# A two-branch memory-attention kernel: first weights in two transfers, later betas, one copy per memory-update tile, a new table by slot

## The chip, the cores and the metric

The kernel runs on one core of one Trainium2 chip. A core has a matrix engine (TensorE, "PE" in the profile, with its weight loads as "PEld"), VectorE ("DVE"), ScalarE ("ACT"), GpSimd ("POOL") and SyncE ("SP"), which here only issues transfers. The metric is device time of one launch in microseconds (us); lower is better. Times of several runs are given as their median.

## The reference: what is computed

Two branches, A and B, read the same input x (2048 tokens by 640 features, float32) and have weights of their own. Each cuts the tokens into four segments of 512 and has 32 heads of 20 features. A per-token gate mixes the two outputs.

```python
for s in range(N):                       # N = 4 segments of L = 512
    qs, ks, vs = q[:, :, s], k[:, :, s], v[:, :, s]
    logits = einsum("bhqd,bhkd->bhqk", qs, ks) * scale + mask   # mask: -1e9 where key > query
    p = softmax(logits)
    a_dot = einsum("bhqk,bhkd->bhqd", p, vs)
    pq = phi(qs)                         # phi(t) = t + 1 if t > 0 else exp(t)
    a_mem = einsum("bhld,bhde->bhle", pq, M) / (einsum("bhld,bhd->bhl", pq, z)[..., None] + 1e-6)
    outs.append(g * a_mem + (1.0 - g) * a_dot)       # g = sigmoid(beta), one number a head
    pk = phi(ks)
    M = M + einsum("bhld,bhle->bhde", pk, vs)        # the memory's update
    z = z + pk.sum over tokens
# then o @ wo per branch, and  g_token * A + (1 - g_token) * B
```

So a segment's update of the memory (M with z as a 21st column) is needed by the next segment of the same branch, three times in all for each branch.

## The kernel before, in words

**Stages.** A stage t = 0 to 7 is one segment of one branch (branch t % 2, segment t // 2). Its projections q, k and v take 640 x 640 weights, tiled as 5 x 5 blocks of 128; a projection of one 128-feature tile is 15 products, because every float32 operand is split into a high part and a low part and three of the four combinations are kept (high x high, low weight x high, high x low). Attention goes through 8 quads of 4 heads a stage, 64 quads in all. For a quad, "S" units make the scores with queries on the partitions, whose row maxima VectorE takes (line 1275); "T" units make them again with keys on the partitions, with the maxima as two extra rows, and ScalarE takes the exponential (line 1364) and GpSimd cuts the diagonal block (line 1365); a "PV" unit multiplies with v (line 1392).

**The two ways of using the array.** Projections, S, T, transposes (line 973) and memory reads (line 931) use 64 rows of the array, so two instructions run side by side, one in each half; the planner keeps one queue for each half. PV units and the memory's updates (line 1031) use all rows and 32 columns, four side by side, and both halves have to come to a stop for them. The first two projections (q tile 0 and k tile 0, `job_head`, line 870) and the last ones (line 1217) use the full array.

**The memory's update** (`updates` and `updated`). After a PV unit up to three feature tiles m are updated together: 4 token blocks x 4 windows of 32 features a tile, all three tiles side by side in one PSUM bank of 512 columns, 7 or 8 heads x 21 columns a tile (147 or 168). A window of 32 features meets only 2 or 3 heads, so 42 or 63 columns. VectorE then copies each window out of PSUM (line 1052, four copies a tile), to `mbd` in the first segment and to a scratch tile `mt` (there are two) in later ones; GpSimd zeroes what belongs to other heads (`keep_own_heads`, lines 377 and 381) and, in later segments, adds `mt` to `mbd` (line 1057). The bank is given back when the last of its tiles has been copied. 30 tiles are updated in all, in 12 batches of two or three.

**What sets the order.** The order of all instructions is made while the program is built, by a planner that keeps a model of the engines with a cost for every operation: `put(engine, cost, emit, then, prio)` queues an operation, `dma(...)` a transfer on SP's queue, `Store.want` and `give` hand out buffers (8 PSUM banks, 35 rows of 128 x 512, 3 staging tiles `wst`, 4 pairs `wh`/`wl` of split weights). On the chip each engine runs its own list in order and waits by semaphore, so an operation that takes longer than its cost delays all that stands behind it. The planner counts 0.44 for the copies of one updated tile (in `updated`) and `UPD` = 63 / 1200 + 0.0027 for each of the 8 steps of its products. `RULES` holds one line for each of 66 slots (a slot is about one quad): the order in which the slot's five S and five T units come, and seven numbers: how the units are spread over the slot (`span`), when late work may start (`calm`, `wait`), delays between the two halves (`lag`, `wait2`), how many rows must be free (`room`) and how early the slot begins (`hold`).

**The head of the program.** PE starts with `WARM` = 9 idle products on a zeroed tile (line 356). SP issues, in this order, the whole weight tile of q 0 (320 KB), x tile 0 (256 KB), the weight tile of k 0, x tiles 1 and 2, the two branches' betas, and then x tiles 3 and 4, which reuse rows of x that have been split. ACT rounds each arrival to its high part (lines 559 and 604), DVE makes the low part (lines 557 and 609), and `job_head` multiplies whatever is there. When the betas have come, `head_gates` runs their sigmoids: a chain that goes from ACT to DVE and back twice (lines 644, 645 and 651). GpSimd meanwhile sets constants (`small_tiles`, `ones_tiles`), and zeroes the ten `mbd` and two `mt` tiles (line 373).

Of the kernel before, what the change touches and what calls it, by code (L numbers as in the profile page):

```python
# [18 lines left out]
P = 128  # L19
D = 640  # L20
# [22 lines left out]
def tile_gated_mix_infini_attn(  # L43
# [314 lines left out]
    def warm_up():  # L358

        nc.vector.memset(r32(qst[0][:, 0, :]), 0.0)  # L360
        for _ in range(WARM):
            idle_step()

    WARM = 9

    def ones_tiles():
        for t in vst:
# [1400 lines left out]
    for k in range(KT):  # L1768
        if k < len(HEAD0):
            stage(k)  # L1770
# [88 lines left out]
```

## Time and profile before

| what | value |
|---|---|
| median of 3 runs | 998.64 us (998.44 to 998.71) |
| the profiled execution's own time | 997.83 us |
| its span | 996.1 us |
| busy: PE, PEld, DVE, ACT, POOL | 979.4, 821.2, 814.0, 654.4, 604.5 us |
| PE's products with half the array on projections (line 820) | 5400 |
| copies out of PSUM for updates (line 1052) | 120, of 206 ns on average |

A line of a list of groups or of a timeline names the source line, the engine, the operation, the tile written and the tiles read, the shape and the count; in square brackets stands how long the engine had been idle before, and what ended that. A line of the waits reads: engine and line that waited, what it waited for, total us, times, longest. PE's busy time is the union of overlapping, pipelined products, so a busy PE may still have one half of the array empty.

### The profile page before, as it was taken

To read this page: it belongs to the slowest core of one execution; us is meant where nothing else is said; L and a number is where in the kernel's file an instruction comes from. 1 tells how busy PE (TensorE), PEld (TensorE's weight loads), DVE (VectorE), ACT (ScalarE), POOL (GpSimd) and SP (SyncE) were. 2 spreads that over 40 slices of the span, in tenths; PEclk is the share of its full clock that TensorE was granted. 3 is DMA by queue.
4 is the path that set the end of the run, shared out by engine and by line. 5 is a ranking of instruction groups with operands and counts; after the bars stand their busy time and mean duration, and the time that the engine had idled before them with its cause. 6 is when DMAs were issued, how large, how long until landed. Compare 5 with 4: busy or idle time off the path is not lost.

```text
span 996.1 us, 31535 instructions
## 1 busy us (share of the span) xinstructions
PE 979.4 (98%) x11559; PEld 821.2 (82%) x11559; DVE 814.0 (82%) x2904; ACT 654.4 (66%) x1310; POOL 604.5 (61%) x1052
## 2 busy tenths in 40 slices
PE   9999999999999999999999999999999999999998
PEld 7987888778897888987888877889788987879776
DVE  4796978887798977897879988888788997799874
ACT  5366777676586667685685746776577575675572
POOL 5455656766466765675654676576656664666561
PEclk9999999999999999999999999999999999999999
DMA  7987889898797876976759796789667987887521
GB/s 248 311 281 237 291 234 299 261 279 262 239 307 238 272 214 202 319 241 187 225 173 311 212 283 199 211 270 269 195 214 226 295 279 217 239 251 209 142 90 65
DMA packets 146453, 236.47 MB, mean 237 GB/s; under 512 B 12949, under 2 KB 45882, under 8 KB 145978
## 3 DMA queue, kind: packets, MB, share of 16 engines
q1 hardware_dynamic: 146298, 234.46, 76.4%
q8 instruction: 91, 1.49, 0.6%
q14 instruction: 64, 0.52, 0.2%
HBM read 145.26 MB, written 94.65 MB: 241 GB/s over the span
## 4 chain that ended last, share of the span: by engine, by line
PE 84%; DVE 7%; DMA 4%; issue 2%; POOL 2%; SPq 1%; ACT 1%; DVEq 0%; ACTq 0%; POOLq 0%
PE bank L820 51%; PE bank L1392 13%; PE bank L1288 7%; PE bank L1372 7%; PE bank L973 2%; PE bank L931 2%; DMA row<-dots 1%; DVE mt L1052 1%; DVE bank L1275 1%; DVE mbd L1052 1%; PE bank L1031 1%; DMA row<-rowg 1%; DMA dots<-row 1%; DMA kd<-row 1%; DVE mr L1311 1%
## 5 line engine op out<-in xcount | busy, mean ns | idle before, releaser
L1275 DVE CUSTOM_DVE_ANT_0 bank<-bank,tri 128x384 f32<-128x384 f32 (+3 forms) x1024 | 474.4, 520 | 86.6 <-PE bank L1288 75.0
L820 PE MATMUL bank<-row,wh 64*128 64x512 f32 x2308 | 479.7, 402 | 0.2
L1364 ACT ACTIVATE p<-bank 128x512 f32<-128x512 f32 x550 | 301.5, 605 | 141.5 <-PE bank L1372 113.4
L820 PEld LDWEIGHTS bank<-row,wh 64*128 64x128 f32 x2308 | 308.6, 185 | 16.8 <-PE bank L820 1.8
L1365 POOL TENSOR_SCALAR_AFFINE_SELECT p<-p 128x128 f32<-128x128 f32 (+1 forms) x550 | 203.4, 378 | 188.3 <-ACT p L1364 171.6
L820 PE MATMUL bank<-row,wl 64*128 64x512 f32 x1154 | 292.7, 398 | 0.0
L557 POOL TENSOR_TENSOR wl<-wst,wh 128x640 fp32r<-128x640 f32 x115 | 180.5, 1578 | 61.5 <-ACT wh L559 49.3
L1288 PE MATMUL bank<-kst,qst 60*128 60x384 f32 (+3 forms) x1024 | 174.2, 317 | 6.6 <-DVE mt L1052 2.8
L820 PEld LDWEIGHTS bank<-row,wl 64*128 64x128 f32 x1154 | 172.2, 185 | 7.7 <-issue 1.0
L1372 PE MATMUL bank<-qst,kst 62*128 62x128 f32 (+3 forms) x1024 | 172.8, 319 | 2.3 <-DVE mt L1052 0.9
L820 PE MATMUL bank<-wvh,row 64*128 64x320 f32 (+1 forms) x1280 | 166.0, 312 | 0.6 <-DVE row L770 0.6
L1275 DVE DVE_READ_ACCUMULATOR2_ANT mx<- 128x1 f32 x1024 | 144.4, 141 | 0.2
L1288 PEld LDWEIGHTS bank<-kst,qst 60*128 60x128 f32 x1024 | 128.3, 185 | 18.6 <-DVE mbd L1052 3.9
L820 PEld LDWEIGHTS bank<-wvh,row 64*128 64x128 f32 x1280 | 140.7, 185 | 3.1 <-DVE row L770 0.9
L1392 PE MATMUL bank<-p,vst 128*32 128x384 f32 (+3 forms) x1840 | 141.8, 423 | 0.0
L1372 PEld LDWEIGHTS bank<-qst,kst 62*128 62x128 f32 x1024 | 127.8, 186 | 17.0 <-DVE mx L1275 3.9
L1392 PEld LDWEIGHTS bank<-p,vst 128*32 128x32 f32 x1840 | 57.4, 110 | 82.2 <-issue 58.7
L559 ACT CAST wh<-wst 128x640 fp32r<-128x640 f32 x119 | 86.2, 744 | 34.2 <-PE bank L820 18.8
L820 PE MATMUL bank<-wvl,row 64*128 64x320 f32 (+1 forms) x640 | 99.4, 311 | 0.0
L820 PEld LDWEIGHTS bank<-wvl,row 64*128 64x128 f32 x640 | 80.7, 186 | 0.6 <-issue 0.4
L1311 DVE STREAM_TRANSPOSE mr<-mt 32x32 f32<-32x32 f32 x256 | 51.0, 199 | 26.9 <-POOL mt L1300 24.2
L1423 ACT COPY row<-bank 128x512 f32<-128x512 f32 x58 | 34.4, 594 | 56.4 <-PE bank L1392 51.5
(121 smaller groups left out, 1146.2 us busy)
## 6 DMA issues: line engine op xcount, KB each, us to landing
qst<-qd SPq DMA_DIRECT2D x128, 240.0 KB
kst<-kd SPq DMA_DIRECT2D x128, 240.0 KB
qd<-row SPq DMA_DIRECT2D x40, 512.0 KB
kd<-row SPq DMA_DIRECT2D x40, 512.0 KB
dots<-row SPq DMA_DIRECT2D x56, 256.0 KB
wst<-wmix SPq DMA_DIRECT2D x35, 320.0 KB
row<-dots SPq DMA_DIRECT2D x42, 256.0 KB
qd<-row SPq DMA_DIRECT2D x40, 256.0 KB
```

The source lines that it names most:

```text
L557: put(lo_eng, lo_cost, lambda: lo.tensor_tensor(out=wl, in0=w3, in1=r32(wh), op=ALU.subtract), end, prio=3)
L559: put("A", 0.625, lambda: nc.scalar.copy(wh, w3), low, prio=6)
L820: return nc.tensor.matmul(bank_of, lhsT=w[ROWS[half]], rhs=x_[ROWS[half]], start=start, stop=stop)
L931: return nc.tensor.matmul(pm[:, a - h0:c - h0, :].rearrange("p h e -> p (h e)"), lhsT=r32(pqTs[t, m][ROWS[half], P * n:P * (n + 1)]), rhs= ...
L1275: put("D", w / 960.0 + 0.105, lambda: nc.vector.tensor_tensor_reduce(out=sc[:, off:off + w], in0=sc[:, off:off + w], in1=tri[:, L - w:], s ...
L1288: lane_ops[half].append((mm(w), lambda pair=pair, qb=qb, off=off, w=w, r=r, sc=sc: nc.tensor.matmul(sc[:, off:off + w], lhsT=q[r, pair, P ...
L1311: nc.vector.transpose(r32(mr[:, 32 * j:32 * j + 32]), r32(mt[32 * j:32 * j + 32, :]))
L1364: put("A", 0.483, lambda: nc.scalar.activation(pt, sc, AF.Exp, scale=SCALE), lambda: (bank.give(sc), put("G", 0.15 + 0.105 * len(todo), la ...
L1365: "G", 0.15 + 0.105 * len(todo), lambda: nc.gpsimd.affine_select(out=blocks, in_=blocks, pattern=[[0, len(todo)], [1, P]], base=0, channel ...
L1372: lane_ops[half].append((mm(w), lambda pair=pair, kb=kb, off=off, w=w, r=r, sc=sc: nc.tensor.matmul(sc[:, off:off + w], lhsT=k[r, pair, P ...
L1392: nc.tensor.matmul(po[32 * j:32 * j + 32, P * kb:], lhsT=vst[t % 2][:, kb, h * E1:h * E1 + 32], rhs=pts[i, n, f][0][:, off:off + w], start ...
L1423: either(0.483, lambda: nc.scalar.copy(r32(oT), po), 0.605, lambda: nc.vector.tensor_copy(r32(oT), po), end, 2)
```

## The change

- **Weights of the head in two transfers each.** `head_weights` brings k-block 0 of a tile (128 x 128, 64 KB) by itself, into a row, and blocks 1 to 4 (256 KB) into a staging tile. SP's order is now: q 0 first piece, x tile 0, k 0 first piece, q 0 rest, x tile 1, k 0 rest, x tile 2, x tiles 3 and 4. Each piece is split by itself. `job_head` takes its weights from `head_hi` and `head_lo`; the rows go back when a projection is done.
- **Two idle products fewer**: `WARM` = 7.
- **The betas** are asked for at 16.0 of the planner's clock, not at the start. Their chain of sigmoids moves with them.
- **One copy for each updated tile**: the whole tile (128 partitions x 147 or 168 columns) is copied at once, whatever the other heads' places in PSUM hold, and `keep_own_heads` zeroes those as before. The copy is counted at 0.22, `UPD` at 0.047, and the twelve tiles are no longer zeroed at the start (`ones_tiles` is counted at 1.6, not 2.8).
- **All 66 lines of `RULES` but one are new.** The planner makes another order from them, on every engine; what is multiplied is the same.

```diff
-        1: "SSTSTSTSTT 1.01 2.38 0.34 8 1.4 1.6 1",
+        1: "TSTSTSTSTS 1.01 2.38 0.3 8 0 1.6 1.12",
...
-    WARM = 9
+    WARM = 7
...
-        for t in (*mbds[0], *mbds[1], *mt_store.free):
-            nc.gpsimd.memset(t, 0.0)
...
+    def head_weights(i, part):
+        t, kind, m = jobs[i]
+        src = weights[t % 2][kind][m]
+        staged.add(i)
+
+        def split_from(w3, wh, wl, us, hi_us, lo_us, end):
+            def landed():
+                def low():
+                    head_hi[i, part] = wh
+                    put("D", lo_us, lambda: nc.vector.tensor_tensor(out=wl, in0=w3, in1=r32(wh), op=ALU.subtract), end, prio=3)
+
+                put("A", hi_us, lambda: nc.scalar.copy(wh, w3), low, prio=6)
+
+            cols = slice(0, 1) if part == 0 else slice(1, KT)
+            dma(us, lambda: nc.sync.dma_start(out=w3, in_=src[:, cols, :]), landed, prio=0, lat=1.1)
+
+        if part == 0:
+            def got_rows(*rows):
+                head_rows[i] = rows
+                st, wh, wl = (x[:, :P].rearrange("p (k n) -> p k n", k=1) for x in rows)
+
+                def end():
+                    head_lo[i, 0] = wl
+
+                split_from(r32(st), wh, wl, 0.25, 0.2, 0.2, end)
+
+            big.want((F32, F32R, F32R), got_rows)
+            return
...
-    UPD = 63 / 1200.0 + 0.0027
+    UPD = 0.047
...
-        def take(dst):
-            for r, a, c in windows(m):
-                h = slice(a - LO[m], c - LO[m])
-                nc.vector.tensor_copy(dst[r, h, :], v[r, h, :])
...
-            put("D", 0.44, lambda: take(tmp), lambda: (
+            put("D", 0.22, lambda: nc.vector.tensor_copy(tmp[:, :nh, :], v), lambda: (
...
-            put("D", 0.44, lambda: take(mbd), lambda: (
+            put("D", 0.22, lambda: nc.vector.tensor_copy(mbd, v), lambda: (
...
-    for k in range(KT):
-        if k < len(HEAD0):
-            stage(k)
+    for i in (0, 1):
+        head_weights(i, 0)
+        if i == 0:
+            want_x(0, 0)
+    for i in (0, 1):
+        head_weights(i, 1)
+        want_x(0, 1 + i)
+    for k in (3, 4):
         want_x(0, k)
...
-        dma(0.9, lambda b=b: nc.sync.dma_start(out=bts[b], in_=betas[b].partition_broadcast(P)), betas_there, prio=15)
+        at(16.0, lambda b=b: dma(0.9, lambda: nc.sync.dma_start(out=bts[b], in_=betas[b].partition_broadcast(P)), betas_there, prio=15))
```

**How the order changes.** Engine lists are shown in program order, with the line of the kernel (of the changed one, where lines moved: 870 became 909, 820 became 858, 1275 became 1310, 1052 became 1094 and 1099).

On ACT before, at the head of the program: the beta chain (`gmem`, `gdot`, `gcol`, line 644) stands ahead of the rounding of x tiles 3 and 4.

```order
L604 CAST row_25_197<-row_6_190 128x512
L644 ACTIVATE gmem_92<-beta_199 128x32
L644 ACTIVATE gdot_94<-beta_199 128x32
L644 ACTIVATE gcol_132<-gcol_132 128x1
L644 ACTIVATE gmem_93<-beta_200 128x32
L644 ACTIVATE gdot_95<-beta_200 128x32
L644 ACTIVATE gcol_133<-gcol_133 128x1
L604 CAST row_72_233<-row_4_188 128x512
L604 CAST row_77_236<-row_7_191 128x512
```

On ACT now, from its first rounding on: the two small weight pieces (written to rows 10 and 21), the two larger ones (`wh`), and all five x tiles (line 642), with nothing else between them.

```order
L582 CAST row_10_191<-row_9_190 128x128
L642 CAST row_16_194<-row_4_186 128x512
L582 CAST row_21_197<-row_20_196 128x128
L582 CAST wh_145<-wst_142 128x512
L642 CAST row_29_199<-row_5_187 128x512
L582 CAST wh_147<-wst_143 128x512
L642 CAST row_37_201<-row_6_188 128x512
L642 CAST row_84_222<-row_4_186 128x512
L642 CAST row_89_225<-row_7_189 128x512
```

The six instructions of the beta chain have gone from between the third and the fourth x tile; they now stand behind the second k projection's evacuation.

On DVE before, at the update of tiles 2, 3 and 4 in the first segment of branch A: eleven rows for the twelve copies and, behind them, the first row maximum of the next S unit.

```order
L1052 COPY mbd_2_72<-bank_141 32x63
L1052 COPY mbd_2_72<-bank_141 32x42 x2
L1052 COPY mbd_2_72<-bank_141 32x63
L1052 COPY mbd_3_73<-bank_141 32x42
L1052 COPY mbd_3_73<-bank_141 32x63
L1052 COPY mbd_3_73<-bank_141 32x42 x2
L1052 COPY mbd_4_74<-bank_141 32x63
L1052 COPY mbd_4_74<-bank_141 32x42
L1052 COPY mbd_4_74<-bank_141 32x63
L1052 COPY mbd_4_74<-bank_141 32x42
L1275 ISA bank_137,mx_1640<-bank_137,tri 128x512
```

On DVE now, at the same update:

```order
L824 TENSOR_TENSOR row_1510_1510<-bank_135,row_1509_1509 128x512
L1346 STREAM_TRANSPOSE mr_161<-mt_1531 32x32 x4
L1099 COPY mbd_2_72<-bank_137 128x168
L1099 COPY mbd_3_73<-bank_137 128x147
L1099 COPY mbd_4_74<-bank_137 128x147
L1310 ISA bank_137,mx_1614<-bank_137,tri 128x512
```

Twelve copies have become three, and the bank that the next S unit takes is the one that they empty.

On PE before, ahead of the fourth PV unit from the end: two projections (banks 2 and 0) side by side, one in each half of the array, and an S unit (banks 7 and 1) in both halves.

```order
L820 MATMUL bank0_134<-row23_17920_15547,wh3_151 128x512
L1288 MATMUL bank7_141<-kst2_86,qst2_82 128x256
L1288 MATMUL bank1_135<-kst2_86,qst2_82 128x256
L1288 MATMUL bank7_141<-kst2_86,qst2_82 128x256
L1288 MATMUL bank1_135<-kst2_86,qst2_82 128x256
L820 MATMUL bank2_136<-row23_17920_15547,wl2_150 128x512
L820 MATMUL bank0_134<-row23_17920_15547,wl3_152 128x512
L820 MATMUL bank2_136<-row5_17921_15548,wh2_149 128x512
L820 MATMUL bank0_134<-row5_17921_15548,wh3_151 128x512
L820 MATMUL bank2_136<-row12_17934_15560,wh2_149 128x512
```

On PE now, at about the same place (bank 6 collects a projection, bank 1 transposes of the memory's output O, banks 3 and 0 a T unit):

```order
L858 MATMUL bank6_140<-row19_18077_15553,wh1_147 128x512
L858 MATMUL bank6_140<-row19_18077_15553,wl1_148 128x512
L1013 MATMUL bank1_135<-ident_68,O0_157 128x64 x4
L858 MATMUL bank6_140<-row14_18078_15554,wh1_147 128x512
L858 MATMUL bank6_140<-row7_18044_15528,wh1_147 128x512
L858 MATMUL bank6_140<-row7_18044_15528,wl1_148 128x512
L1407 MATMUL bank3_137<-qst0_80,kst0_84 128x256 x2
L1407 MATMUL bank0_134<-qst0_80,kst0_84 128x256 x2
L858 MATMUL bank6_140<-row26_18045_15529,wh1_147 128x512
L858 MATMUL bank6_140<-row34_18061_15541,wh1_147 128x512
```

Here one projection's products follow each other in one half of the array, with four short transposes as their only company in the other.

More of the change, by code (lines that the diff above doesn't have):

```diff
@@ L554, in split_hi @@
                 wh, wl = pair
-                def low():
-                    split_hi_[i] = pair
-                    put(lo_eng, lo_cost, lambda: lo.tensor_tensor(out=wl, in0=w3, in1=r32(wh), op=ALU.subtract), end, prio=3)
-                put("A", 0.625, lambda: nc.scalar.copy(wh, w3), low, prio=6)
+                put("A", 0.625, lambda: nc.scalar.copy(wh, w3), lambda: put(
+                    lo_eng, lo_cost,
+                    lambda: lo.tensor_tensor(out=wl, in0=w3, in1=r32(wh), op=ALU.subtract), end, prio=3), prio=6)
                 def end():
@@ L570, in stage, with got, end @@
         wst.want(1, got, prio=i)
+    head_hi, head_lo, head_rows = {}, {}, {}
+    def head_weights(i, part):
[19 more added lines that the diff above has]
+            return
+        def got(w, pair):
+            def end():
+                wst.give(w)
+                split[i] = pair
+                head_lo[i, 1] = pair[1][:, 1:, :]
+            w3 = w.rearrange("p (k n) -> p k n", n=P)
+            split_from(w3[:, 1:, :], pair[0][:, 1:, :], pair[1][:, 1:, :], 0.84, 0.52, 0.62, end)
+        wst.want(1, lambda w: whl.want(1, lambda pair: got(w, pair), prio=i), prio=i)
     mixed_there = set()
@@ L856, in there @@
             k, i, j = x
-            return i in (split if j == 1 else split_hi_) and (0, k) in (xs if j == 2 else x_hi)
+            return (i, min(k, 1)) in (head_lo if j == 1 else head_hi) and (0, k) in (xs if j == 2 else x_hi)
         while todo:
@@ L874, in job_head @@
             if n[i] == 3 * KT:
+                big.give(*head_rows.pop(i))
                 after_whole(qk_finish(*jobs[i], pps[i]))
```

9 lines of the change are left out of this document (5 added, 4 removed), and 128 rows, old and new, of the table RULES.

## The prediction

> **What bounds the kernel now.** I read the page first, then the busy time by window, the waits of PE, the lines that copy updates out of PSUM, and timelines of one update and of the head. The page's span and busy times, and one window:
>
> ```profile
> span 996.1 us, 31535 instructions
> PE 979.4 (98%) x11559; PEld 821.2 (82%) x11559; DVE 814.0 (82%) x2904; ACT 654.4 (66%) x1310; POOL 604.5 (61%) x1052
> ...
> 30.00:60.00 30.00, 30.00 (x299) 28.56 (x297) 26.08 (x105) 15.40 (x35) 13.09 (x17) 1.00 0.92 297
> ```
>
> PE has something in flight in all but 17 us, so nothing but PE can set the end, and a microsecond that PE saves early is kept: the window from 30 to 60 shows no idle time in which it could get lost. But "busy" is a union; one half of the array may be empty in it. What PE waited for (engine and line, released by, total us, times, longest):
>
> ```profile
> PE bank L1288 <- DVE mt L1052: 2.8, 3, 1.2
> PE bank L1288 <- DVE mbd L1052: 2.8, 3, 1.7
> ...
> PE bank L1288 <- DVE row L776: 1.0, 1, 1.0
> PE bank L1372 <- DVE mt L1052: 0.9, 2, 0.5
> PE bank L870 <- ACT row L604: 0.8, 2, 0.6
> PE bank L820 <- DVE row L770: 0.6, 1, 0.6
> PE bank L1372 <- DVE mbd L1052: 0.6, 1, 0.6
> ```
>
> Of the 9.5 us in these rows, line 1052, the copies of updates, holds 2.8 + 2.8 + 0.9 + 0.6 = 7.1, and line 604, x in the head, 0.8. Both are what the change touches. One update of three tiles, in the timeline (start, length, engine, line, tiles, count; in brackets the idle time before and its releaser):
>
> ```profile
> 92.40 1.36 PE L1031 MATMUL bank<-vst,row 128*32 128x63 f32 x96
> ...
> 93.84 2.67 DVE L1052 COPY mbd<-bank 32x63 f32<-32x63 f32 x12 [3.38 <-PE bank L1031]
> ...
> 96.56 0.30 PEld L1288 LDWEIGHTS bank<-kst,qst 60*128 60x128 f32 x4 [2.12 <-DVE mbd L1052]
> 96.56 0.50 PE L1288 MATMUL bank<-kst,qst 60*128 60x384 f32 x4 [1.69 <-DVE mbd L1052]
> ```
>
> The planner counted 3 x 0.44 = 1.32 for these twelve copies and got 2.67. It had promised the bank to an S unit (line 1288), and PE stood 1.69 until the last copy.
>
> **The copies (term 1).** Durations of DVE operations that read PSUM, by group (busy us, mean ns), and a later update, whose third tile needs a scratch tile back from GpSimd:
>
> ```profile
> L948 DVE TENSOR_TENSOR O<-bank,mw 128x320 f32<-128x320 f32 x48 | 23.6, 491 | 1.7
> ...
> L1052 DVE COPY mt<-bank 32x42 f32<-32x42 f32 (+1 forms) x80 | 16.5, 206 | 8.4 <-PE bank L1031 4.8 <-issue 1.2 <-POOL mbd L1057 0.7
> ...
> L989 DVE COPY row<-bank 128x512 f32<-128x512 f32 x6 | 4.1, 689 | 2.0 <-PE bank L973 2.0
> ```
>
> ```profile
> 468.54 0.54 POOL L1057 TENSOR_TENSOR mbd<-mbd,mt 128x168 f32<-128x168 f32 x1
> ...
> 469.11 0.93 DVE L1052 COPY mt<-bank 32x63 f32<-32x63 f32 x4 [0.73 <-POOL mbd L1057]
> ...
> 470.10 0.44 PE L1288 MATMUL bank<-kst,qst 60*128 60x384 f32 x1 [0.99 <-DVE mt L1052]
> ```
>
> From 320 to 512 columns the time grows by (689 - 491) / 192 = 1.03 ns a column, so a copy of 147 columns should take about 491 - 173 x 1.03 = 313 ns and one of 168 about 335, by estimate. Three take 0.96, not 2.67: 1.7 earlier, which is the longest wait. In a later segment the third copy still waits for GpSimd; there the first copy ends 0.93 - 0.31 = 0.6 earlier and so does GpSimd's work, and the third is 0.6 shorter: 1.2 earlier, again the longest wait of `mt`. Had the order stayed, all 7.1 would go. What may stay: the planner now counts 0.22 for what should take 0.31 to 0.34, so a batch of three is still promised 0.3 too early; over the 9 stops of the four rows that is 2.7 at most, and 4.4 are saved. What may be saved beyond: the weight loads of one half waited longer than PE as a whole.
>
> ```profile
>   PEld bank L1288: 7.5, 6
> ...
>   PEld bank L1372: 2.8, 4
> ```
>
> That is 10.3 in all. So the copies give -7.1, within -4.4 and -10.3; I take the row of PE itself. DVE is freed of 120 x 0.206 - 30 x 0.32 = 15 us, and what comes late next at such a place is GpSimd's zeroing, which no row shows PE waiting for. The smaller `UPD` only moves the planner's clock: 96 products took 1.36, so 0.43 to 0.45 a tile, beside 8 x 0.055 = 0.44 counted before and 8 x 0.047 = 0.38 now. That promises a bank up to 0.2 earlier a batch, and is in the 2.7.
>
> **The head (term 2).** PE's idle products (line 356), the head's products (line 870), and what ACT and SP did:
>
> ```profile
> 3.39 2.33 PE L356 MATMUL bank<-qst 128*128 128x512 f32 x5
> 5.88 0.80 PE L870 MATMUL bank<-row,wh 128*128 128x512 f32 x1 [0.16 <-ACT row L604]
> ...
> 6.90 1.21 PE L870 MATMUL bank<-row,wh 128*128 128x512 f32 x4
> ...
> 10.53 0.40 PE L870 MATMUL bank<-row,wh 128*128 128x512 f32 x1
> 11.53 0.50 PE L870 MATMUL bank<-row,wh 128*128 128x512 f32 x1 [0.60 <-ACT row L604]
> ...
> 12.56 0.86 PE L870 MATMUL bank<-row,wh 128*128 128x512 f32 x3
> ```
>
> ```profile
> 0.81 0.38 SPq L568 DMA_DIRECT2D wst<-in_a_wq_dram  x1
> ...
> 1.25 0.42 SPq L624 DMA_DIRECT2D row<-in_xT_dram  x1
> ...
> 4.10 0.73 ACT L559 CAST wh<-wst 128x640 fp32r<-128x640 f32 x1 [2.02 <-DMA wst<-in_a_wq_dram]
> ...
> 5.21 0.62 ACT L604 CAST row<-row 128x512 fp32r<-128x512 f32 x1 [0.38 <-DMA row<-in_xT_dram]
> ...
> 8.02 0.23 ACT L644 ACTIVATE gmem<-beta 128x32 f32<-128x32 f32 x1
> ...
> 9.97 0.20 ACT L644 ACTIVATE gcol<-gcol 128x1 f32<-128x1 f32 x1 [1.60 <-DVE gcol L651]
> ...
> 10.87 1.12 ACT L604 CAST row<-row 128x512 fp32r<-128x512 f32 x2
> ```
>
> x tile 0 (256 KB) was there 1.11 after the 320 KB ahead of it. With 64 KB ahead it should come 1.1 earlier: rounding at 4.1, PE's first product at 4.8, not 5.88. Seven idle products cover that: the nine end at about 5.5, two fewer at 4.7. At first PE is slow: five idle products in 2.33 are 0.42 apart, while three of the head at 12.56 are (0.86 - 0.40) / 2 = 0.23 apart; the four from 6.90 are (1.21 - 0.40) / 3 = 0.27 apart, so the change falls near 7.1. Before it three products had started (5.88 to 6.90), now six: 3 x 0.23 = 0.7 saved. Second, the stop from 10.53 to 11.53: x tiles 3 and 4 were rounded at 10.87, behind the beta chain, which held ACT from 8.02 and waited 1.60 for DVE in it. Without it a step of 0.23 remains: 0.8 saved, if the tiles have landed. They were asked for when x tile 0's row was free, so they too come 1.1 earlier, at 9.8 at the latest, rounded by 10.4; PE would want them at about 10.1. Term 2 is -1.5; without the second part -0.7, with both unreduced (1.1 + 0.8) -1.9.
>
> The Trainium skill (TensorE: Matmul & The Clock Gate, "What's actually happening") says that PE's clock is gated to half until one free-running window of about 3.4 us has been busy, and falls back after an idle one. The spacings, 0.42 and then 0.23, agree with it; by that rule fewer idle products are no gain, and a gap after them a risk (a rival below).
>
> The beta chain now stands on ACT and DVE behind the second k projection, about 3 us long, with two weight roundings and that projection's own low part behind it on their queues. Before, the first of those roundings stood idle for its transfer:
>
> ```profile
> 25.05 0.73 ACT L559 CAST wh<-wst 128x640 fp32r<-128x640 f32 x1 [0.67 <-DMA wst<-in_a_wq_dram]
> ```
>
> So ACT has slack there, PE is full with projections (the window from 30 to 60 above), and I count nothing; if the cover fails, PE waits for that rounding, 3 - 0.67 = 2.3 at worst, and I leave 0.5 of it in the range. The 12 zeroings taken from GpSimd were behind everything that PE needs. The gate's small transfer keeps its place behind the weights; its products stand at the end of the head.
>
> **The table (term 3).** PE's order has the same products as before, two idle ones aside, so the table can only change how well the two halves are filled. Two rows each of full projections price a product in one half:
>
> ```profile
> 20.29 1.33 PE L820 MATMUL bank<-row,wl 64*128 64x512 f32 x10
> ...
> 21.46 1.32 PE L820 MATMUL bank<-row,wh 64*128 64x512 f32 x10
> ...
> 24.86 1.99 PE L820 MATMUL bank<-wvh,row 64*128 64x322 f32 x24
> ...
> 26.68 0.91 PE L820 MATMUL bank<-wvl,row 64*128 64x322 f32 x10
> ```
>
> Ten of 512 columns take 1.17 in two halves, 0.234 each in its half; 24 of 322 take 1.82, 0.152 each. That is 0.011 + 0.00044 x columns. Adding this up in PE's order for each half between two PV units, the fuller half exceeds the mean of both by 4.6 us in all before, and by 8.1 now; 2.4 of the difference lies in the two stretches ahead of the fourth and third PV unit from the end, where one projection runs alone. So +3.5 at most by this count. At the other end: kinds of instruction change inside a half 2615 times, not 2661, and if each change costs 0.1 (no row isolates it), that is 46 x 0.1 / 2 = -2.3; a table made for the new costs may also leave out the other stops of the waits (1.0 + 0.6), so -4. I take +1.5: I halve the count and round down, because a half that is thin in the order may be so at a place where PE would have waited anyway.
>
> **Sum.** -7.1 - 1.5 + 1.5 = -7.1. The profiled execution took 997.83 (span 996.1 and 1.7 around it): 990.7. The median of the runs, 998.64, is 0.8 above it: 991.5.
>
> **The rivals.** (a) *The bank is still late.* The third copy of a batch stands on DVE waiting for GpSimd, with the row maxima of the next S unit behind it; for it is the 0.73 above, and a DVE order in which the next S unit takes the very bank; against it, that stop was part of the waits already counted. Half of term 1 stays: 991.5 + 3.6 = 995.1. (b) *The clock opens a window later,* since x comes after the seven idle products end and PE pauses. Eight more products at 0.42 in place of 0.23 cost 8 x 0.19 = 1.5, so 993.0; against it, transfers should be there at 4.1. By the Trainium skill's window (the same page and section), half speed for 3.4 us more, it would be 1.7 by estimate. (c) *The table fits better than the count says,* its -4 end: 991.5 - 5.5 = 986.0. (d) *Slower: the new order bunches units at the end of the program,* where few projections are left, and PE stops for PSUM banks that DVE's maxima or ACT's exponentials hold. A stop costs up to 1.7 (the longest above). Eight of them in the last ten stretches make 13.6: 991.5 + 13.6 = 1005. From five stops on (7.1 / 1.7 = 4.2) the change is a loss. For it: the two thin stretches, DVE at 82%. Against: the freed 15 us of DVE. (e) That a copy of 128 partitions costs four times one of 32 is excluded by line 948, 128 partitions at 491 ns.
>
> **How the numbers follow.** Forecast 0.62, (a) 0.13, (b) 0.05, (c) 0.08, (d) 0.12. The time is the forecast's. Its own range, from the terms' ends not all at once, is 987 to 996. With (a) to (c) and the far end of term 1 (3.2 more) in part, the range is 985 to 997.5; it leaves out (d) and all far ends at once. A measurement of this kernel tells about 0.2%, 2.0 us, from no change: faster is below 996.6, slower above 1000.6. Faster: 0.62 x 0.97 + 0.13 x 0.75 + 0.05 x 0.9 + 0.08 = 0.82. Slower: (d) in two of three cases, 0.08. Same: 0.10.
>
> **What would show it.** PE's first head product near 4.8 and no stop of a microsecond ahead of x tile 3; lines 1094 and 1099 at about 320 ns each and gone from the list of what PE waits for, or below 1 us in all; PE's waits otherwise at 4 us or less. I am wrong if the new order brings waits of another kind that add up to more than 3 us, if the copies take over 0.5, or if the head's first product stays near 5.9.

## The result, and the profile after

The changed kernel took 991.81 us (median of 4, 990.02 to 994.29) beside 998.67 us for the kernel before (998.44 to 999.74): a ratio of 0.9931 [0.9907, 0.9955]. Timed again beside the last two experiments it took 993.61 us, 0.9949 [0.9937, 0.9962]. The forecast was 991.5. The experiments show that this was luck: two errors cancelled, one of 7 us and one of 8 to 9. The copies alone are worth 14 us, and the rest of the change costs 8 to 9.

The profiled execution, 994.29 us, was the slowest of its four. Its page, and after it the list of what PE waited for as a whole (engine and line, released by, total us, times, longest):

```profile
span 992.5 us, 31438 instructions
...
PE 981.9 (99%) x11557; PEld 824.9 (83%) x11557; DVE 804.1 (81%) x2826; ACT 648.1 (65%) x1299; POOL 603.5 (61%) x1043
```

```profile
PE bank L356 <- DVE qst L360: 1.5, 1, 1.5
PE bank L1013 <- issue: 1.4, 1, 1.4
PE bank L909 <- ACT row L642: 0.9, 2, 0.7
PE bank L1323 <- DMA kst<-kd: 0.9, 1, 0.9
PE bank L1323 <- ACT p L1399: 0.5, 2, 0.4
PE bank L971 <- DVE mx L1310: 0.4, 1, 0.4
```

The copies have left the list, as forecast. PE's span shrank by 3.6 us, yet it is busy 2.5 us longer than before with two products fewer. That is a first hint that a busy PE has got emptier. A second profile of the same kernel shows it too: 982.1 busy in a span of 991.3.

The copies of the kernel after by group, and one of its updates in the timeline:

```profile
L1094 DVE COPY mt<-bank 128x147 f32<-128x147 f32 (+1 forms) x20 | 5.5, 310 | 10.2 <-PE bank L1071 8.3 <-POOL mbd L1092 1.9
...
L1099 DVE COPY mbd<-bank 128x147 f32<-128x147 f32 (+1 forms) x10 | 2.6, 309 | 5.1 <-PE bank L1071 5.1
```

```profile
92.16 1.36 PE L1071 MATMUL bank<-vst,row 128*32 128x63 f32 x96
...
93.67 0.77 DVE L1099 COPY mbd<-bank 128x168 f32<-128x168 f32 x3 [1.21 <-PE bank L1071]
...
94.49 0.26 PEld L1323 LDWEIGHTS bank<-kst,qst 60*128 60x128 f32 x2 [0.52 <-DVE mbd L1099]
```

A copy takes 310 and 309 ns (forecast 313 to 335). But copies in a row overlap: each starts 0.22 to 0.25 us after the one before. So three take 0.77 (forecast 0.96), where the new planner counts 0.66, and a batch of two takes 0.53, where it counts 0.44. A batch is promised only 0.1 too early. The products of three tiles still take 1.36, and the weight load of the next S unit waits for the last copy: 0.52, no longer 2.12, but not nothing.

The head of the kernel after in the timelines of PE and of ACT:

```profile
4.77 2.23 PE L909 MATMUL bank<-row,row 128*128 128x512 f32 x6
7.68 0.51 PE L909 MATMUL bank<-row,wh 128*128 128x512 f32 x1 [0.68 <-ACT row L642]
...
8.31 1.20 PE L909 MATMUL bank<-row,wh 128*128 128x512 f32 x4
...
11.18 0.50 PE L909 MATMUL bank<-row,wh 128*128 128x512 f32 x1 [0.26 <-ACT row L642]
...
14.27 0.39 PE L909 MATMUL bank<-row,wh 128*128 128x512 f32 x1
```

```profile
7.01 0.62 ACT L642 CAST row<-row 128x512 fp32r<-128x512 f32 x1 [0.59 <-DMA row<-in_xT_dram]
...
10.50 1.26 ACT L642 CAST row<-row 128x512 fp32r<-128x512 f32 x2 [1.63 <-DMA row<-in_xT_dram]
```

PE starts at 4.77 (forecast 4.8), and then stands for x tile 1 and again for x tiles 3 and 4, which ACT had to wait 1.63 us for. The last product of the head starts at 14.27; in the kernel before it did so at 14.19:

```profile
14.19 0.40 PE L870 MATMUL bank<-row,wh 128*128 128x512 f32 x1
```

So the head gained nothing in this profile. Its end differs from run to run: with the old head the last product started at 13.74 to 14.29 in five profiles of different kernels, and in the second profile of the kernel after at 13.73. No gain shows over that spread.

### The profile page after: what moved, and what is told of

Read it like the earlier page. It is cut to its first block, busy times and chain, and to the rows that moved or that the text cites. A ratio compares the mean times of both kernels' runs of the same rounds, so it can differ in the third digit from the quotient of the medians.

```text
span 992.5 us, 31438 instructions
## 1 busy us (share of the span) xinstructions
PE 981.9 (99%) x11557; PEld 824.9 (83%) x11557; DVE 804.1 (81%) x2826; ACT 648.1 (65%) x1299; POOL 603.5 (61%) x1043
## 4 chain that ended last, share of the span: by engine, by line
PE 92%; DMA 3%; DVE 3%; issue 1%; ACT 1%; SPq 0%; ACTq 0%; DVEq 0%
PE bank L858 55%; PE bank L1427 14%; PE bank L1323 8%; PE bank L1407 8%; PE bank L971 3%; PE bank L1013 2%; PE bank L1071 1%; DMA kst<-kd 1%; DMA row<-in_xT_dram 1%; DMA beta<-in_b_beta_dram 1%; DMA kd<-row 1%; DVE bank L1310 1%; PE bank L1252 0%; DMA qd<-row 0%; DVE row L1237 0%
## 5 line engine op out<-in xcount | busy, mean ns | idle before, releaser
L858 PE MATMUL bank<-row,wh 64*128 64x512 f32 x2308 | 485.9, 402 | 0.1
L858 PEld LDWEIGHTS bank<-row,wh 64*128 64x128 f32 x2308 | 313.0, 185 | 16.6 <-PE bank L858 0.9
L1400 POOL TENSOR_SCALAR_AFFINE_SELECT p<-p 128x256 f32<-128x256 f32 (+1 forms) x544 | 199.6, 377 | 183.0 <-ACT p L1399 169.8
L858 PE MATMUL bank<-row,wl 64*128 64x512 f32 x1154 | 297.3, 398 | 0.0
L858 PE MATMUL bank<-wvh,row 64*128 64x320 f32 (+1 forms) x1280 | 179.4, 313 | 0.0
L1407 PE MATMUL bank<-qst,kst 62*128 62x384 f32 (+3 forms) x1024 | 171.9, 317 | 0.1
L1323 PE MATMUL bank<-kst,qst 60*128 60x384 f32 (+3 forms) x1024 | 170.1, 319 | 1.7 <-DMA kst<-kd 0.9
L858 PEld LDWEIGHTS bank<-wvh,row 64*128 64x128 f32 x1280 | 148.8, 185 | 1.6 <-issue 0.6
L1427 PE MATMUL bank<-p,vst 128*32 128x512 f32 (+3 forms) x1816 | 139.5, 424 | 0.0
L1323 PEld LDWEIGHTS bank<-kst,qst 60*128 60x128 f32 x1024 | 124.3, 186 | 14.8 <-issue 2.0
```

Source lines behind the costliest of these rows:

```text
L858: return nc.tensor.matmul(bank_of, lhsT=w[ROWS[half]], rhs=x_[ROWS[half]], start=start, stop=stop)
L1323: lane_ops[half].append((mm(w), lambda pair=pair, qb=qb, off=off, w=w, r=r, sc=sc: nc.tensor.matmul(sc[:, off:off + w], lhsT=q[r, pair, P ...
L1400: "G", 0.15 + 0.105 * len(todo), lambda: nc.gpsimd.affine_select(out=blocks, in_=blocks, pattern=[[0, len(todo)], [1, P]], base=0, channel ...
L1407: lane_ops[half].append((mm(w), lambda pair=pair, kb=kb, off=off, w=w, r=r, sc=sc: nc.tensor.matmul(sc[:, off:off + w], lhsT=k[r, pair, P ...
L1427: nc.tensor.matmul(po[32 * j:32 * j + 32, P * kb:], lhsT=vst[t % 2][:, kb, h * E1:h * E1 + 32], rhs=pts[i, n, f][0][:, off:off + w], start ...
```

## The experiments

### One copy per tile in the old order

```diff
-            for r, a, c in windows(m):
-                h = slice(a - LO[m], c - LO[m])
-                nc.vector.tensor_copy(dst[r, h, :], v[r, h, :])
+            nc.vector.tensor_copy(dst[:, :nh, :], v)
```

This is the kernel before with nothing else changed: same table, same counts, same head, same order on every engine.

> The kernel before, with its own order of work, its old table and its old head; only the copies of an updated tile out of PSUM are one each instead of one per head's window. The planner still reckons 3 x 0.44 = 1.32 us for a batch whose copies should now take about 0.96, so no bank is promised too early. My theory (the copies were waited for, and nothing else takes their place): 998.6 - 7.1 = 991.5, ratio 0.993, and neither mt nor mbd stands in the list of what PE waits for with more than 0.5 us. Rival, the bank is late anyway because GpSimd's zeroing and adding stand behind the copies: half of it, 995 (0.9965). Rival, the gain of the change came from the new table: no more than 2 us here, 997 (0.998).

Measured: 983.88 us, 0.9859 [0.9845, 0.9872]. That is 14 us, twice my theory, and better than the whole change. Its page, and the update that the prediction showed for the kernel before, in the timeline:

```profile
span 982.2 us, 31441 instructions
...
PE 973.5 (99%) x11559; PEld 823.6 (84%) x11559; DVE 792.7 (81%) x2814; ACT 653.7 (67%) x1310; POOL 602.9 (61%) x1052
```

```profile
91.18 1.36 PE L1031 MATMUL bank<-vst,row 128*32 128x63 f32 x96
...
92.63 0.77 DVE L1050 COPY mbd<-bank 128x168 f32<-128x168 f32 x3 [3.39 <-PE bank L1031]
...
93.45 0.30 PEld L1286 LDWEIGHTS bank<-kst,qst 60*128 60x128 f32 x4 [0.22 <-DVE mbd L1050]
93.45 0.50 PE L1286 MATMUL bank<-kst,qst 60*128 60x384 f32 x4
```

The same 11559 products keep PE busy 5.9 us less (979.4 to 973.5), and its idle time falls by 8.0 (from 996.1 - 979.4 = 16.7 to 8.7). Nearly all of the 5.9 lies in the stretches with an update, busy by the page, and in no list of what PE waited for. I read it as time in which one half of the array stood for the bank while the other half worked. That is not shown, since no view keeps the halves apart. There is another reading: a product's record is longer than the distance to the next product (0.39 beside 0.23 us in the head), so every stop also adds a tail that counts as busy.

Since both kernels have the same order, the starts of their PV units can be subtracted one by one. The difference grows almost only around the updates and stays nearly flat between them, and it is 14.0 us at the 63rd of the 64. Six of the 12 batches have three tiles and ran over their promise by 2.67 - 1.32 = 1.35. The other six have two tiles, whose eight copies took 1.76 for 0.88. Together that is 6 x 1.35 + 6 x 0.88 = 13.4, about the 14.0 that were paid. (This counts the copies' own time. In later segments the third copy of a batch waits for GpSimd as well, with one copy a tile as with four.) Against the planner's own clock (the time its code holds when it places a PV unit) the picture is plain. Chip minus planner, us:

```
PV unit                    1st   11th   31st   41st   63rd
planner, old table        62.2  194.8  494.1  643.9  959.6
  before                   0.8    6.2    8.7   11.2   14.5
  one copy                 0.4    0.1   -0.8   -0.8    0.5
  copied twice             0.8    2.9    3.7    4.5    6.6
planner, new table        65.2  192.1  498.1  642.8  955.1
  after                    3.0    3.8    6.9   10.0   11.1
  after, second run        2.1    2.8    4.1    8.8   10.0
  after, thin copies       1.9    1.8    2.7    6.7    7.8
  the same, fewer products 3.4    2.4    3.0    4.7    5.5
```

With one copy the chip follows the plan to within 1 us through 960 us. The kernel before fell behind it by 14.5, and the kernel after falls behind its own plan by 10 to 11 again.

### Each tile copied twice

```diff
             nc.vector.tensor_copy(dst[:, :nh, :], v)
+            nc.vector.tensor_copy(dst[:, :nh, :], v)
```

> The kernel before with one copy per updated tile, and that copy made twice in a row (the same data, no result changes). Three tiles then hold DVE for 6 x 0.31 = 1.87 us where the planner promises 3 x 0.44 = 1.32: late by 0.55 a batch, after 1.35 with the four copies (2.67) and -0.36 with one. The theory now (what counts is by how much a batch runs over what the planner promised, nearly all of it is paid, 14.0 us for 12 batches that ran over by 1.35): 12 x 0.55 = 6.6, less the 0.18 a batch that the 14.0 fell short of 12 x 1.35, so 4.4 to 6.6 above the 983.9 of one copy: 988.3 to 990.5, ratio 0.9904 to 0.9926. Rival (PE has projections to fill in, only a lateness of about a microsecond is felt): within 1 us of one copy, 0.985 to 0.987.

Measured: 989.95 us, 0.9912 [0.9897, 0.9928], inside the theory's 0.9904 to 0.9926; the rival is out. The same update in its timeline:

```profile
93.17 0.33 DVE L1050 COPY mbd<-bank 128x168 f32<-128x168 f32 x1 [3.38 <-PE bank L1031]
...
94.68 0.31 DVE L1051 COPY mbd<-bank 128x147 f32<-128x147 f32 x1
...
95.05 0.30 PEld L1287 LDWEIGHTS bank<-kst,qst 60*128 60x128 f32 x4 [1.28 <-DVE mbd L1051]
95.05 0.50 PE L1287 MATMUL bank<-kst,qst 60*128 60x384 f32 x4 [0.84 <-DVE mbd L1051]
```

Six copies end 1.8 us after the first began, where 1.32 was promised, and the S unit that was given the bank is late. The four copies of a batch of two took 1.22 for 0.88, so the batches ran over by 6 x 0.50 + 6 x 0.34 = 5.0 in all, and 6.1 were paid. (My theory had taken all twelve batches for batches of three, here and for the 14.0.) What a batch costs is by how much it runs over its promise, even when that is half a microsecond.

### Four copies in the new order

The kernel after with the four windows of a tile copied singly again, and the scratch tiles zeroed at the start.

```diff
-            put("D", 0.22, lambda: nc.vector.tensor_copy(mbd, v), lambda: (
+            put("D", 0.22, lambda: take(mbd), lambda: (
```

> The kernel after in its own order, but each updated tile is copied window by window again (and the scratch tiles are zeroed at the start, as that needs). The planner reckons 3 x 0.22 = 0.66 us for a batch whose copies take 2.7, so banks are promised 2.0 us too early, 1.35 before the change. My theory (the copies decide): the 7.1 us of waits come back and grow by the difference of promises, about 0.65 x 9 stops = 6, so between +7 and +13 on the 991.8 of the kernel after: 999 to 1005, ratio to the kernel before 1.000 to 1.006. Rival (the table or the head made the gain, copies matter little): below 995, ratio under 0.9965.

Measured: 1008.71 us, 1.0108 [1.0094, 1.0122]. That is 15 to 17 us above the kernel after, more than expected. A batch of three now runs over by 2.67 - 0.66 = 2.0, one of two by 1.76 - 0.44 = 1.3, together 20, and the chip ends 24.6 us behind the planner at the 63rd PV unit. The copies decide in the new order too.

### The old table under the new counts, and 0.43 for 0.44

The kernel after with the 66 lines of the old table, and nothing else:

```diff
-        1: "TSTSTSTSTS 1.01 2.38 0.3 8 0 1.6 1.12",
+        1: "SSTSTSTSTT 1.01 2.38 0.34 8 1.4 1.6 1",
...
```

> The kernel after with the old table of order and spacing by slot; costs, head, betas and copies stay as changed. My theory from counting lanes (the new table costs 1.5): 990.3, ratio 0.9916. Rival 1 (the table was made for the new costs and pays): 993 or more, ratio above 0.9943, with more waits of PE than the kernel after has. Rival 2 (a table only scatters the order; any table gives the same): within 1 us of the kernel after, 0.9921 to 0.9941.

Measured: 1064.64 us, 1.0660 [1.0637, 1.0683]. My theory and rival 2 fall. Rival 1 holds by its words, 993 us or more with more waits of PE (27 us idle by the page, 10.6 in the kernel after), but nobody had 70 us. The planner's own clock says it too: 1041.5 at the end, beside 978.4 with the new table and 979.1 for the kernel before. What the engines did there, by windows (length; busy us and count of PE, PEld, DVE, ACT, POOL; granted clock, DMA share, GB/s), and the line of its page:

```profile
120.00:125.00 5.00, 5.00 (x67) 5.00 (x64) 4.45 (x22) 4.85 (x10) 3.88 (x7) 1.00 1.05 358
...
135.00:140.00 5.00, 5.00 (x51) 5.00 (x49) 0.00 (x0) 0.83 (x2) 0.00 (x0) 1.00 0.02 3
...
165.00:170.00 5.00, 4.69 (x41) 4.19 (x37) 0.00 (x0) 0.00 (x0) 0.50 (x1) 1.00 1.00 237
```

```profile
PE 1036.3 (97%) x11557; PEld 856.5 (81%) x11557; DVE 799.5 (75%) x2828; ACT 649.5 (61%) x1301; POOL 600.4 (56%) x1039
```

In the windows from 135 and from 165 PE runs 51 and 41 products in 5 us instead of 67, with DVE and ACT nearly idle, and yet counts as busy for 5.00 and 4.69 us. I read that as projections without attention work to pair with. A change of one count by 0.01 does the same to the other table. One copy in the old order, counted at 0.43 (in both places):

```diff
-            put("D", 0.44, lambda: take(mbd), lambda: (
+            put("D", 0.43, lambda: take(mbd), lambda: (
```

> One copy per updated tile in the old order's table, but the planner counts 0.43 us for it instead of 0.44, nothing else. By its own clock the planner now ends at 1032.1 instead of 979.1: the table's numbers were found for 0.44, and everything behind the first update is placed anew. Theory (a table belongs to one set of counts; the chip follows the planner's clock): 983.9 + 53 = 1037, ratio 1.035 to 1.042. Rival (the planner's clock is wrong for such a plan, the chip hardly notices): 984 to 995, ratio under 0.997.

Measured: 1052.04 us, 1.0518 [1.0494, 1.0541]: 68 us for a hundredth of a microsecond in a count. The theory holds in kind, but the time lies above its range: the chip stays within 0.7 us of the plan for the first 24 PV units and falls behind later. So each of these tables belongs to the one set of counts that it was found for, and the worth of "the table alone" cannot be measured by swapping it.

### Shorter copies and fewer products in the new order

```diff
-            put("D", 0.22, lambda: nc.vector.tensor_copy(mbd, v), lambda: (
+            put("D", 0.22, lambda: nc.vector.tensor_copy(mbd[:, :1, :], v[:, :1, :]), lambda: (
...
-            for n in range(NB):
+            for n in range(NB - 1):
```

The first pair of lines (and its like for `mt`) makes the thin copies; the second kernel has both pairs.

> The kernel after in its own order, but each copy of an updated tile takes only the first head's 21 columns of 147 or 168 (the rest of the update is left out, so the memory is not the reference's), and the scratch tiles are zeroed at the start. By 1.03 ns a column the copy should take 0.31 - 0.13 = 0.18 us, under the 0.22 that the planner promises. The theory now (the promise of 0.22 is what costs the kernel after its gain): three copies end 0.39 us earlier, about 12 batches, so 4 to 5 us gained on the kernel after, 987 to 988, ratio 0.989. Rival (the copies are out of the way already, and the loss against one copy in the old order is the new table's filling of the halves): within 1 us of the kernel after, 0.992 to 0.994.

> As the thin copies, and of an update's four products per head window only three are made (a quarter of the update's sum is left out too). 96 products took 1.36 us, 0.45 a tile, where the planner now counts 8 x 0.047 = 0.376; 72 should take 1.02, 0.34 a tile. The theory (both promises are too short): 30 tiles x 0.11 = 3.4 less work on PE beyond the thin copies' gain, 983.5 to 985, ratio 0.986, and PE no longer falls behind the planner's clock at the updates; of the 11 us by which the kernel after ends behind that clock only the 3 of the head and the first stretch are left. Rival (table): 3.4 less work and nothing else, 988.4, ratio 0.990.

Measured: 990.92 us, 0.9924 [0.9911, 0.9936], and 987.71 us, 0.9899 [0.9883, 0.9915]. Both lie where the rival put them. By the medians the thin copies gain 0.9 to 2.7 us (on the kernel after's two times), and the 3.4 us of products left out gain 3.2 more (2.5 by the ratios). The copies did fall under the promise (groups of the thin copies' kernel):

```profile
L1096 DVE COPY mt<-bank 128x21 f32<-128x21 f32 x20 | 2.9, 176 | 10.4 <-PE bank L1073 8.3 <-POOL mbd L1094 1.9 <-issue 0.2
```

So the short promise of the copies is between a tenth and a third of the 8 to 9 us that the kernel after lost. That agrees with what whole copies run over: 6 x 0.11 + 6 x 0.09 = 1.2. The theory had missed that copies in a row overlap. The lag behind the planner between the first and the 63rd PV unit tells the rest: 8 in the kernel after, 6 with thin copies, 2 with fewer products as well. But of that last step 3.4 is work that was really removed; the planner was short of it by 30 x (1.36 / 3 - 0.376) = 2.3.

### The head and the betas

The kernel after, with every instruction in its place but the betas: their transfers go out at the planner's time 50, their chain runs at 64.

```diff
+    at(50.0, lambda: [nc.sync.dma_start(out=bts[b], in_=betas[b].partition_broadcast(P)) for b in range(2)])
+    at(64.0, head_gates)
```

> The kernel after, each instruction in its place but two groups: the two transfers of beta are issued at the planner's time 50 instead of 16, and the chain of gates that reads them stands at 64 on the engines. In the trace of the kernel after, the issue of the betas took SP 1.19 + 0.85 us, and the second landed at 25.9; the S unit of the second half pair began at 44.26 behind a wait for its k tile's transfer, 42.00 in the kernel before. My theory (the betas' place holds up the k tile that goes through DRAM): that S unit starts about 2 us earlier and 1 to 2.5 us are gained, 989.3 to 990.8, ratio 0.9907 to 0.9922. Rival, PE has other work there and loses nothing: same as the kernel after, 991.8 (0.9931). Rival, the chain at 64 meets the maxima of the softmax on DVE and ACT: 1 to 2 us slower than after.

Measured: 993.93 us, 0.9958 [0.9946, 0.9971], no better than the kernel after. In the kernel after, the S unit of the second half pair started late, behind its k tile:

```profile
44.26 0.77 PE L1323 MATMUL bank<-kst,qst 60*128 60x512 f32 x5 [0.94 <-DMA kst<-kd]
```

In this experiment it started at 43.47 with no stop. That need not come from the betas: in the second profile of the kernel after, with nothing moved, it started at 43.28 and had no stop either. And the chain now held ACT ahead of the first PV unit (two rows of its timeline):

```profile
68.05 0.20 ACT L682 ACTIVATE gcol<-gcol 128x1 f32<-128x1 f32 x1 [0.35 <-DVE gcol L689]
...
68.62 0.64 PE L1427 MATMUL bank<-p,vst 128*32 128x512 f32 x4 [1.12 <-ACT vst L1129]
```

A second try put the chain where ACT is idle and gave x tiles 3 and 4 space of their own.

```diff
+    x_fresh = {3: 0, 4: 1}
+            st = O_store.free[0][:, x_fresh[k], :L] if not s and k in x_fresh else row
...
+    at(30.0, lambda: [nc.sync.dma_start(out=bts[b], in_=betas[b].partition_broadcast(P)) for b in range(2)])
+    at(41.5, head_gates)
```

> The kernel after, each instruction in its place but for two things: x tiles 3 and 4 of the head are staged in space of their own, so that their transfers are issued without a wait for rows to come free (SP stood 2.66 us for them); and the two beta transfers are issued at the planner's time 30 and their chain runs at 41.5, where ACT has 5 us free. Theory for the head (the wait for rows is what made x tiles 3 and 4 late, landed at 10.5): both are rounded by 9.8, the head's last product starts 0.5 to 0.8 earlier than 14.27. Rival for the head (the transfers share the queues, an earlier issue only makes them share sooner): landed at 10.2 or later, no gain. For the betas: the S unit of the second half pair starts by 42.5 instead of 44.26, nothing else waits. Together 1.5 to 2.5 us: 989.3 to 990.3, ratio 0.991 to 0.992; by the rival less than 1 us.

Measured: 993.55 us, 0.9949 [0.9935, 0.9962]: nothing gained. The timelines of ACT and of PE in its head:

```profile
8.14 0.62 ACT L582 CAST wh<-wst 128x512 fp32r<-128x512 f32 x1 [0.68 <-DMA wst<-in_a_wk_dram]
8.78 0.62 ACT L646 CAST row<-row 128x512 fp32r<-128x512 f32 x1
9.44 1.31 ACT L646 CAST row<-O 128x512 fp32r<-128x512 f32 x2
```

```profile
14.21 0.39 PE L913 MATMUL bank<-row,wh 128*128 128x512 f32 x1
```

x tiles 3 and 4 are rounded 1.06 us earlier (9.44), as the theory said, and the head ends at 14.21 instead of 14.27, as the rival said: the rest of k's weights came later in exchange (rounded at 8.14, not 7.64). But one profile says little here. In the second profile of the kernel after, unchanged, the two tiles were rounded from 9.97 and the head ended at 13.73. The S unit started at 42.67, 1.6 earlier than in the kernel after, and the first PV unit at 67.90, only 0.3 earlier. In seven runs of this order that PV unit lay anywhere from 66.4 to 68.6. My theory of the betas falls with it: there was a stop (0.94), but not in every run, and moving the betas gained no time.

### Both kernels again, and the best one

> The kernel after once more, unchanged, on the chip that runs the two below, for a narrower interval: 990 to 994, ratio 0.991 to 0.9955. If the first stretch's loss hangs on when the second beta lands, this profile's first PV unit lies anywhere from 66.4 to 68.6 us.

Measured: 993.61 us, 0.9949 [0.9937, 0.9962]; the first PV unit at 67.23. Its profile shows a stop of PE of 1.91 us, the longest in it. Four more runs of this order have that stop at 1.4 us or more, the kernel after's first profile has it at 0.4, and the one with fewer products not at all. ACT waits for a transfer to free a row, and the exponentials behind it hold a bank (timelines of ACT and of PE):

```profile
642.57 0.58 ACT L1029 COPY row<-bank 128x512 f32<-128x512 f32 x1 [2.74 <-DMA kd<-row]
643.05 1.09 ACT L1399 ACTIVATE p<-bank 128x512 f32<-128x512 f32 x2
```

```profile
643.70 0.51 PE L1323 MATMUL bank<-kst,qst 60*128 60x256 f32 x4 [1.91 <-ACT p L1399]
```

> One copy per updated tile in the old order, and the twelve zeroings of scratch tiles at the start left out, as the change does: the whole of what the change does to the copies, without its new counts, head and table. The zeroings are behind everything that PE needs: same as with them, 983 to 985, ratio 0.985 to 0.987, and 0.7 to 0.8% below the kernel after. Rival (the zeroings hold up GpSimd's first low parts): 1 us less.

Measured: 984.20 us, 0.9852 [0.9837, 0.9867]. The zeroings cost nothing, as forecast. This is the change's whole treatment of the copies in the old order, and it beats both kernels: by 14 us the kernel before, by 8 to 9 the kernel after.

## Why the prediction was right, and where it was wrong

**The copies (-7.1, forecast -4.4 to -10.3): right in kind, wrong in size.** Alone they give -14. The step that failed is "I take the row of PE itself": the list holds only time in which neither half of the array ran. Even the far end, the waits of the weight loads, was too small. What decides is by how much a batch overran its count: 1.35 for six batches of three and 0.88 for six of two, 13.4 together, and 14.0 were paid. The 2.67 and 1.32 of a batch of three stood in the prediction. One more step was off, without harm: "Three take 0.96" adds up single copies, and three in a row took 0.77.

**The new counts (said to be inside 2.7): they cost some 3 to 5.** By the experiments 0.9 to 2.7 of it are the copies (0.77 taken, 0.66 counted), and 2.3 the products (0.45 taken, 0.376 counted a tile). I treated both as a bank promised too early. For the products that was wrong: they are PE's own time, and a plan that leaves them out ends late by all of it.

**The head (-1.5): nothing came of it.** First, x tiles 3 and 4 "at 9.8 at the latest, rounded by 10.4" failed: ACT waited for their transfers and began to round them at 10.50, and at 9.97 in the second profile. In the first profile PE also stood 0.68 for x tile 1, a stop that the prediction did not have. Second, in the experiment even x tiles at 9.44 brought no gain, as another transfer was late instead. I read that as pieces in another order with the same sum. The DMA engines were busy 87% and 85% of the time in the first stretches, at 255 and 260 GB/s (windows of the kernel after; the last two columns are DMA share and GB/s):

```profile
2.00:6.00 4.00, 4.00 (x10) 2.70 (x10) 1.19 (x3) 1.39 (x5) 3.93 (x8) 1.00 0.87 255
6.00:10.00 4.00, 3.33 (x13) 2.21 (x13) 2.63 (x4) 2.28 (x4) 1.32 (x9) 1.00 0.85 260
```

The Trainium skill (Perfetto Trace Analysis, "DMA Optimizations") says that splitting transfers may let some start sooner, and may let the whole finish sooner if the DMA engines are generally idle. The traces agree with the first: the first product came at 4.77 and 4.89, beside 5.52 to 6.18 in five profiles with the old head. For the second they show only the other case: with engines that were not idle, the head ended no sooner.

**The betas (counted at nothing): right in the sum.** A stop behind them stands in one of the two profiles of the kernel after (0.94), and moving the betas gained no time.

**The table (+1.5): not a term by itself.** The count of the fuller half, 8.1 against 4.6, said nothing: the planner's clock, which knows both halves, ends at 978.4, 0.7 earlier than before. The step that failed is "the table can only change how well the two halves are filled". It also sets which transfer is due when: the stop near 643, behind a transfer, is in no profile of the old order. Of the 8 to 9 us between one copy in the old order and the whole change, the lags give 1 to 3 to the first stretch (2.1 and 3.0 at the first PV unit, against 0.4 to 0.9 in the old order), some 3 to 5 to the counts, 0.7 and 2.2 (in its two runs) to the stop near 643, and the plan itself -0.7. The first and the third of these shares are read off the table of lags; no run takes them apart. Some 2 us of lag stay even with thin copies and fewer products, and what makes them is open.

**The signs.** The first product at 4.77, the copies at 310 ns and gone from the list, PE's other waits at 4.1 without the idle products' start: nearly all came out, and yet two sums were wrong, by 7 and by 8 to 9 us. Signs taken from the list that misled the estimate could not show its error. Rival (a), a bank still late, was partly true: a weight load still waited 0.52 for a copy. Rivals (b) and (d) did not occur: the four products from 8.31 are (1.20 - 0.39) / 3 = 0.27 apart, as fast as four at that place before, and PE's stops did not bunch at the end.

## What to carry to other kernels

Where the array is used in halves, the idle time of PE and its list of waits can be far below what a late operand costs (7.1 listed, 14.0 paid here). Compare what the schedule promised with what the operations take, batch by batch, and add up. Operations in a row can overlap, so measure the whole batch and not one of them. Keep a planner's counts at or above the measured times: the copy counted at 0.44 that took 0.31 cost nothing, while counts below the measured times made the plan lag. A hand-tuned table and its counts were one object here, so put a cheaper operation first into the old order unchanged, and measure that before tuning anew.

## What the chip showed that I had not expected

A stop of a few microseconds can cost twice. In the kernel counted at 0.43 PE stood two times (timeline):

```profile
285.49 0.27 PE L973 MATMUL bank<-ident,row 64*128 64x64 f32 x1 [3.00 <-DVE row L776]
...
296.12 0.79 PE L1370 MATMUL bank<-qst,kst 62*128 62x512 f32 x1 [4.54 <-DVE O L948]
```

The granted clock, the third number from the right in its windows, fell within two microseconds after work had come back, and stayed at half until 299, through the second stop:

```profile
283.00:285.00 2.00, 0.00 (x0) 0.00 (x0) 2.00 (x3) 0.06 (x1) 0.03 (x1) 1.00 0.98 363
285.00:287.00 2.00, 1.51 (x20) 1.51 (x20) 2.00 (x3) 0.73 (x2) 2.00 (x2) 0.72 1.06 417
287.00:289.00 2.00, 2.00 (x18) 1.95 (x16) 2.00 (x4) 2.00 (x5) 2.00 (x2) 0.50 0.09 37
...
297.00:299.00 2.00, 2.00 (x19) 2.00 (x18) 0.78 (x3) 0.54 (x1) 1.60 (x5) 0.50 1.01 222
299.00:301.00 2.00, 2.00 (x22) 1.21 (x23) 0.00 (x0) 0.00 (x0) 0.00 (x0) 0.87 0.17 33
```

In its profiled execution that kernel's mean clock was 0.973, that of the old table 0.974, all others' 0.998 or more; it may be part of why both end behind even their planners' clocks. The Trainium skill (TensorE: Matmul & The Clock Gate, "What's actually happening") has PE back at half speed after one idle window of about 3.4 us, in windows that run freely. The trace agrees on the half; a stop of 3.00 by the profile was enough here, and no run shows why. The column doesn't show every slow stretch: it reads 1.00 in the window from 2 to 6 of the kernel after, where the idle products were 0.42 us apart.

A copy out of PSUM takes 176 ns for 21 columns, 197 to 198 for 42, 219 for 63, 303 to 306 for 147 and about 330 for 168. Those of 42 and 63 have 32 partitions, the others 128, so the partitions make no difference here: by estimate from these numbers it is some 155 ns and 1 ns a column. Twelve small ones took 2.67 us, one after the other, and three large ones that overlap took 0.77.
